# Attention and projections with split words on one core: order of the weight pieces on ScalarE, first queries by another queue, flag made at step 88

## The chip, the cores and the metric

One core of a Trainium2 chip runs the whole program. The metric is the device time of one execution in microseconds; the time of a kernel is the median over several runs. The core has five engines, each with its own order of instructions that is fixed when the program is built: TensorE (PE, matrix products), VectorE (DVE), ScalarE (ACT), GpSimd (POOL) and SyncE (SP, which here only issues transfers). SP and ScalarE each have a queue for transfers. Engines wait for each other by semaphores; an instruction that waits holds up everything behind it on its engine.

## The reference

Four batches of 768 tokens, eight heads of 64. Attention is local and causal (a token sees itself and the `n_local` - 1 = 95 tokens before it) with the first `n_global` = 8 tokens visible to all, and a bias that falls with distance. Its output, 3072 rows of 512, goes through two products with a GELU between them:

```python
scores = scale * np.matmul(q, k.transpose(0, 1, 3, 2)) + bias
scores = np.where(keep, scores, -1000000000.0)
a = softmax(scores)                       # with 1e-9 in the denominator
x = (a @ v).transpose(0, 2, 1, 3).reshape(3072, 512)
h = x @ w_in                              # 512 -> 2048
g = 0.5 * h * (1.0 + erf(h / sqrt(2)))
out = (g @ w_out).astype(float32)         # 2048 -> 512
```

`n_local`, `n_global`, `w_in` and `w_out` come as 64-bit numbers, so the weights are 16 MB of words.

## The kernel before, in words

The 3072 tokens are cut into 12 chunks of 256 (three to a batch), and the 2048 middle columns into 8 slices of 256. A *step* `T` is one chunk with one slice: `m1` (line 461) multiplies the chunk's `x` with the slice of `w_in` into `h`, `gelu` (lines 471 to 473) takes ScalarE, GpSimd and VectorE in turn, and `m2` (line 491) multiplies with the slice of `w_out` and adds up in `acc`. There are 96 steps. The first 16 take chunks 0 and 1 by turns, slice after slice, so that the weights are needed slowly at first; from step 16 on a chunk takes its eight slices in a row.

Products are made in a fast number format, with each operand split into a high part `h` and a low part `l` and three products added (`wh*xh + wh*xl + wl*xh`). The names in the profile follow this: `winh`, `winl`, `wouth`, `woutl`, `xh`, `xl`, `gh`, `gl`.

**Attention** of a chunk is spread over about ten steps (`att`): scores `s` (line 332 for the first two chunks, called native because their attention isn't split; line 336 for the others), exponentials on ScalarE (line 356), a transpose `t` on TensorE (line 382) that ScalarE copies to `pt` (line 385 or 389), the product `av` with the values (line 410 or 424), and `x`. The attention of chunk 0 and chunk 1 comes ahead of step 0 for the most part. Its loads are kr (keys), qr (queries) and vr (values), for four pairs of heads each, all issued by SP (lines 225 to 229 and 286 to 293). The load of the limits (line 55) stands between them, and the masks `pen` are made from it.

**Weights** come in 32 pieces, four to a slice (two of `w_in`, two of `w_out`), each a transfer of 512 KB (line 156), with four buffers for slices 0 to 6. A piece is turned from 64-bit words into a high and a low part in six operations (`split_weights`, lines 180 to 193):

- ScalarE, line 180: the low words, in place, to integers of a few bits. This is the first ScalarE operation of a piece, and it waits for the load.
- VectorE, lines 182 and 184: bits of the high words into `wb`.
- VectorE, line 186: `wb` and the low words joined. After it the buffer is free, and SP can issue the load of a later piece.
- ScalarE, line 192: the high part `hi` (winh or wouth).
- VectorE, line 193 (the page shows line 151): the low part `lo`.

Slice `s` is split at step `DECODE[s]` (-6, -4, ... 8) in the order of the program text. That text isn't the order of the engines: a planner orders each engine's instructions when the program is built, by when it thinks their inputs are ready and then by their place in the text. `after` (line 134) gives it an extra edge between two instructions. Such an edge is an order, not a transfer of data: between two instructions of one engine it becomes no semaphore. The kernel uses it to keep the loads of the weights in order and to keep exponentials and GELUs in order.

**The flag.** The fast path holds only for limits of a certain size, moderate scores and moderate weights. All words of the weights are therefore loaded a second time (`check_load`, `c` in the profile) during steps 16 to 80, and VectorE folds them into `wand` (line 203). At the end `flag` (line 578) folds all conditions into one number `flag_i`: ten small VectorE operations, a TensorE transpose of one column (line 596) and three more VectorE operations. One of its tiles, `wmin`, has the tag "o", whose two buffers are also those of the output tiles. Each engine then reads the number (line 750) and branches (line 751) past the general path, which isn't run on these inputs.

Of the kernel before, what the change touches and what calls it, by code (L numbers as in the profile page):

```python
# [10 lines left out]
I32 = mybir.dt.int32  # L11
# [6 lines left out]
P = 128  # L18
# [5 lines left out]
CT = 256  # L24
# [27 lines left out]

def load_scalars(nc, pool, src, name):
    w = pool.tile([P, 2, 2], I32, name=name + "_w")
    nc.sync.dma_start(w.rearrange("p i t -> p (i t)"), src.bitcast(I32).partition_broadcast(P))
    f = pool.tile([P, 2, 2], F32, name=name + "_f")
    nc.vector.tensor_copy(f, w)
    r = pool.tile([P, 2], F32, name=name)
    lo, hi = f[:, :, 0], f[:, :, 1]
    nc.vector.scalar_tensor_tensor(out=r, in0=lo, scalar=0.0, in1=hi, op0=ALU.is_lt, op1=ALU.add)  # L60
    nc.vector.scalar_tensor_tensor(out=r, in0=r, scalar=4294967296.0, in1=lo, op0=ALU.mult, op1=ALU.add)
    return r[:, 0:1], r[:, 1:2]
# [6 lines left out]
class Fast:  # L69
    def __init__(self, tc, ctx, qT, kT, v, w, out, limits):  # L70
        self.tc, self.nc = tc, tc.nc
        self.qT, self.kT, self.v, self.w, self.out = qT, kT, v, w, out
        self.limits = limits
        pool = lambda name, bufs=1, **k: ctx.enter_context(tc.tile_pool(name=name, bufs=bufs, **k))
        self.ctx = ctx
        self.early = ExitStack()
        self.es = self.early.enter_context(tc.tile_pool(name="es", bufs=1, side="right"))
        self.const = pool("const")
        self.wts = pool("wts")
        self.stg = pool("stg", 3)  # L80
        self.kq = pool("kq", 2)
        self.vp = pool("vp", 2)
        self.pp = pool("pp", 4)
        self.ptp = pool("ptp", 2)
        self.xp = pool("xp", 3)
        self.gp = pool("gp", 2)
        self.sm = pool("sm", 2)
        self.words = ExitStack()
        self.ws = self.words.enter_context(tc.tile_pool(name="ws", bufs=4))
        self.ps_acc = pool("ps_acc", 2, space=PSUM)  # L90
        self.ps = pool("ps", 6, space=PSUM)
        self.win, self.wout = {}, {}
        self.kt, self.qt, self.vt, self.raw = {}, {}, {}, {}
        self.pt_n, self.pt_t, self.av, self.x = {}, {}, {}, {}
        self.stat, self.g, self.h = {}, {}, {}
        self.acc, self.t3 = {}, {}
        self.xs = {}
        self.last_table = self.last_word = None

    def consts(self):  # L100
        nc, const = self.nc, self.const
# [65 lines left out]
    def split_weights(self, s):  # L167
        nc = self.nc
        if s == LATE:
            self.early.close()  # L170
            self.wts = self.ctx.enter_context(self.tc.tile_pool(name="wlate", bufs=1, side="right"))
        if s == NST - 1:
            self.words.close()
            self.wts = self.ctx.enter_context(self.tc.tile_pool(name="wlast", bufs=1))
        for nm, dst, shape in (("win", self.win, [P, 4, 256]), ("wout", self.wout, [P, 2, 512])):
            dst[s] = tuple(self.wts.tile(shape, F32R, name=f"{nm}{k}{s}") for k in "hl")
        for i in range(4):
            w = self.raw.pop((s, i, "w"))
            lw, hw = w[:, :, 0], w[:, :, 1]
            nc.scalar.activation(out=lw, in_=lw.bitcast(U32), func=AF.Copy, scale=2.0 ** -29)  # L180
            a = self.sm.tile([P, 512], I32, name=f"wb{s}_{i}", tag="o")
            nc.vector.tensor_scalar(out=a, in0=hw, scalar1=0x07FFFFFF, scalar2=3,
                                    op0=ALU.bitwise_and, op1=ALU.logical_shift_left)
            nc.vector.scalar_tensor_tensor(out=a, in0=hw, scalar=-0x40000000, in1=a,  # L184
                                           op0=ALU.bitwise_and, op1=ALU.bitwise_or)
            nc.vector.tensor_tensor(out=a, in0=a, in1=lw, op=ALU.add)  # L186
            af = a.bitcast(F32)
            if i < 2:
                hi, lo = (x[:, 2 * i:2 * i + 2, :].rearrange("p d f -> p (d f)") for x in self.win[s])
            else:  # L190
                hi, lo = (x[:, i - 2, :] for x in self.wout[s])
            nc.scalar.copy(hi, af)
            self.lo_dve(lo, af, hi)

    def check_load(self, n):
# [19 lines left out]
    def load_qk(self, c, p):  # L215
        nc = self.nc
        b, cc = divmod(c, CPB)
        k0 = (b * H + 2 * p) * D * S
        first = cc == 0
        nb = 1 if first else 2  # L220
        if c in NATIVE:
            kr = self.es.tile([P, nb, 256], F32, name=f"kr{c}_{p}", tag="kn", bufs=4)
            qr = self.es.tile([P, CT], F32, name=f"qr{c}_{p}", tag="qn", bufs=4)
            if first:
                nc.sync.dma_start(kr[:, 0, :], dap(self.kT, k0, [[S, P], [1, 256]]))
            else:
                nc.sync.dma_start(kr[:, :, NG:256], dap(self.kT, k0 + cc * CT - 96, [[S, P], [P, 2], [1, 224]]))
                nc.sync.dma_start(kr[:, :, 0:NG], dap(self.kT, k0, [[S, P], [0, 2], [1, NG]]))
            nc.sync.dma_start(qr, dap(self.qT, k0 + cc * CT, [[S, P], [1, CT]]))
            self.raw[c, p] = (kr, qr, nb)  # L230
            return
        if p == 0 and (cc == 1 or c == len(NATIVE)):
            self.load_glob(b)
        kr = self.stg.tile([P, 2, nb, 256], F32, name=f"kr{c}_{p}", tag="stage", padded_shape=[P, 2, 2, 256])
        qr = self.stg.tile([P, 2, CT], F32, name=f"qr{c}_{p}", tag="qraw", bufs=1)
        for u in (0, 1):
            ps = slice(u * 64, u * 64 + 64)
            if first:
                nc.sync.dma_start(kr[ps, :, 0, :], dap(self.kT, k0, [[S, D], [D * S, 2], [1, 256]]))
            else:  # L240
                for j in range(2):
                    nc.sync.dma_start(
                        kr[ps, :, j, NG:256],
                        dap(self.kT, k0 + cc * CT + j * P - 96, [[S, D], [D * S, 2], [1, 224]]))
            nc.sync.dma_start(qr[ps], dap(self.qT, k0 + cc * CT, [[S, D], [D * S, 2], [1, CT]]))
        self.raw[c, p] = (kr, qr, nb)
# [285 lines left out]
                    if r == rr:  # L532
                        self.exps(c, bt)

    def run(self):
        self.load_qk(0, 0)
        self.consts()
        last = NCH * NST
        for c in NATIVE:
            for p in range(NP):  # L540
                if (c, p) != (0, 0):
                    self.load_qk(c, p)
                self.load_v(c, p)
            if c == 0:
                for s in range(3):
                    self.load_weights(s)
        for s in range(3, NST - 1):
            self.load_weights(s)
        for self.T in range(START[0] - 1, last):
            T = self.T  # L550
            for s in range(NST):
                if T == DECODE[s]:
                    if s == NST - 1:
                        self.load_weights(s)
                    self.split_weights(s)
            if 16 <= T < 80 and T % 2 == 0:
                self.check_load((T - 16) // 2)
            if 18 <= T < 82 and T % 2 == 0:
                self.check_words((T - 18) // 2)
            if 0 <= T + 1 < last:  # L560
                self.m1(T + 1, 0)
            self.att(T, "pt", 0)
            if 0 <= T + 1 < last:
                self.m1(T + 1, 1)
                self.gelu(T + 1)
            self.att(T, "s", 0)
            self.att(T, "pt", 1)
            if T >= 0:
                self.m2(T, 0)
            self.att(T, "av", 0)  # L570
            self.att(T, "s", 1)
            self.att(T, "exp", 0)
            self.att(T, "split", 0)
            if T >= 0:
                self.m2(T, 1)
            self.att(T, "av", 1)
# [164 lines left out]
def body(tc, qT, kT, v, w, limits, out):  # L741
    nc = tc.nc
    w = w.bitcast(I32)
    with tc.tile_pool(name="flagp", bufs=1) as fp:
        flag_i = fp.tile([1, 1], I32, name="flag_i")
        with ExitStack() as ctx:
            fast = Fast(tc, ctx, qT, kT, v, w, out, limits)
            fast.run()
            fast.flag(flag_i)
        fv = nc.values_load(flag_i, min_val=0, max_val=1)  # L750
        with tc.If(fv):
            general(tc, qT, kT, v, w, out, limits)
# [25 lines left out]
```

## Time and profile before

| what | value |
|---|---|
| median of 3 runs | 751.67 us (749.25 to 754.20) |
| profiled execution | 753.28 us |
| its span, from the first to the last instruction | 750.9 us |
| granted TensorE clock, mean | 0.991 |
| busy: TensorE, VectorE, ScalarE, GpSimd | 718.8, 502.2, 355.6, 304.0 us |
| moved by DMA | 80.91 MB |

A row of a timeline gives the start and the duration in microseconds, the engine, the line, the operation, the tile written and the tiles read, their shapes, the number of instructions merged, and in square brackets how long the engine stood idle before it and what released it. An engine's name with a q (SPq, ACTq, PEldq) is its sequencer, which issues transfers, reads registers and branches. In rows with three numbers divided by slashes these are shortest, median and longest in nanoseconds, followed by the start of the first and the last in microseconds. PEld is the load of the stationary operand, which overlaps the products.

### The profile page before, as it was taken

The numbers are of one execution on the slowest core, as the hardware profiler recorded it, in microseconds if no ns is written. First come the engines' busy times: TensorE is split into PE (matmuls) and PEld (weight loads), VectorE is DVE, ScalarE is ACT, GpSimd is POOL, SyncE is SP. The second block draws the span as 40 slices with busy tenths as digits, with TensorE's granted clock in tenths as the row PEclk, the third lists the DMA queues.
The fourth block names the chain that finished last, engine by engine and source line by source line (L and its number), as shares of the span: only waits on it lengthen the run. The fifth ranks groups of instructions, "written<-read, shape, count | busy, mean of one in ns | idle before, by whom it ended". The sixth has DMA issues, their size and how long they took to land.

```text
span 750.9 us, 13415 instructions
## 1 busy us (share of the span) xinstructions
PE 718.8 (96%) x4617; PEld 649.8 (87%) x4617; DVE 502.2 (67%) x1317; ACT 355.6 (47%) x906; POOL 304.0 (40%) x572
## 2 busy tenths in 40 slices
PE   5997989898999999999999999999999999999995
PEld 3776989787999999999889999999889999989984
DVE  6888887756857867856757867856658867633111
ACT  5646545455355355355355355355355455351110
POOL 2220033654544654543544554542533654431010
PEclk9999999999999999999999999999999999999998
DMA  8995523324434434334424434334334431100000
GB/s 245 269 242 176 173 81 113 98 64 120 119 101 137 115 101 127 97 88 132 119 82 136 119 101 122 100 92 124 99 103 117 127 110 43 44 15 1 29 1 32
DMA packets 74395, 80.91 MB, mean 108 GB/s; under 512 B 12368, under 2 KB 63056, under 8 KB 74320
## 3 DMA queue, kind: packets, MB, share of 16 engines
q1 hardware_dynamic: 70864, 73.69, 34.9%
q10 hardware_dynamic: 3456, 6.29, 2.3%
q8 instruction: 38, 0.62, 0.3%
q14 instruction: 37, 0.30, 0.1%
HBM read 73.66 MB, written 6.29 MB: 106 GB/s over the span
## 4 chain that ended last, share of the span: by engine, by line
PE 69%; DMA 10%; DVE 6%; ACT 6%; POOL 4%; issue 2%; SPq 1%; DVEq 0%; POOLq 0%; ACTq 0%
PE acc L491 29%; PE h L461 27%; DMA w<-w 7%; PE av L424 4%; PE s L336 4%; PE t L382 4%; POOL n L369 3%; ACT n L356 3%; DMA c<-w 2%; DMA kr<-kT 1%; POOL gh L145 1%; DVE wb L186 1%; ACT L356 1%; DVE wb L184 1%; ACT gr L471 1%
## 5 line engine op out<-in xcount | busy, mean ns | idle before, releaser
L461 PE MATMUL h<-xh,winh 128*128 128x256 f32 x768 | 219.7, 286 | 0.0
L461 PE MATMUL h<-xl,winh 128*128 128x256 f32 x768 | 218.6, 285 | 0.0
L461 PE MATMUL h<-xh,winl 128*128 128x256 f32 x768 | 217.3, 283 | 0.0
L491 PE MATMUL acc<-wouth,gh 128*128 128x512 f32 x384 | 155.0, 404 | 7.4 <-POOL gh L145 7.4
L491 PE MATMUL acc<-woutl,gh 128*128 128x512 f32 x384 | 152.4, 397 | 0.0
L461 PEld LDWEIGHTS h<-xh,winh 128*128 128x128 f32 x768 | 146.9, 191 | 2.4
L461 PEld LDWEIGHTS h<-xl,winh 128*128 128x128 f32 x768 | 146.9, 191 | 2.1
L461 PEld LDWEIGHTS h<-xh,winl 128*128 128x128 f32 x768 | 146.9, 191 | 0.2
L491 PE MATMUL acc<-wouth,gl 128*128 128x512 f32 x384 | 144.1, 398 | 1.2 <-DVE gl L151 1.2
L151 DVE TENSOR_TENSOR gl<-gr,gh 128x512 fp32r<-128x512 f32 x96 | 68.6, 715 | 92.5 <-POOL gh L145 92.5
L471 ACT ACTIVATE gr<-h 128x512 f32<-128x512 f32 x96 | 57.4, 598 | 149.8 <-PE h L461 109.9
L369 POOL TENSOR_SCALAR n<-n,su 128x256 f32<-128x256 f32 (+1 forms) x160 | 77.5, 504 | 87.7 <-DVE su L361 76.4
L145 POOL TENSOR_SCALAR gh<-gr 128x512 fp32r<-128x512 f32 x96 | 65.4, 681 | 108.9 <-ACT gr L471 108.9
L145 POOL TENSOR_SCALAR vt<-vr 128x256 fp32r<-128x256 f32 (+1 forms) x80 | 34.7, 435 | 154.1 <-DMA vr<-v 79.5
L356 ACT ACTIVATE n<-n,mn 128x256 f32<-128x256 f32 (+1 forms) x192 | 91.8, 480 | 7.8 <-DVE mn L341 7.5
L491 PEld LDWEIGHTS acc<-wouth,gh 128*128 128x128 f32 x384 | 73.2, 191 | 20.3 <-POOL gh L145 9.2
L491 PEld LDWEIGHTS acc<-wouth,gl 128*128 128x128 f32 x384 | 73.0, 190 | 18.2 <-DVE gl L151 2.9
L491 PEld LDWEIGHTS acc<-woutl,gh 128*128 128x128 f32 x384 | 73.2, 191 | 12.5
L431 ACT COPY t<-av 64x256 f32<-64x256 f32 x80 | 29.3, 366 | 99.3 <-PE av L424 98.8
L389 ACT CAST pt<-t 128x512 fp32r<-128x512 f32 (+1 forms) x80 | 44.4, 555 | 65.0 <-PE t L382 59.4
L341 DVE CUSTOM_DVE_ANT_0 n<-s,pen 128x256 f32<-128x256 f32 (+1 forms) x192 | 68.4, 391 | 5.1 <-PE s L336 3.5
L382 PE MATMUL t<-ident,n 128*128 128x128 f32 x352 | 61.2, 295 | 1.3 <-ACT gr L471 0.7
(87 smaller groups left out, 1060.9 us busy)
## 6 DMA issues: line engine op xcount, KB each, us to landing
w<-w SPq DMA_DIRECT2D x32, 512.0 KB, 4.6
c<-w SPq DMA_DIRECT2D x32, 512.0 KB, 3.7
kr<-kT SPq DMA_DIRECT2D x112, 112.0 KB, 2.7
qr<-qT SPq DMA_DIRECT2D x88, 128.0 KB, 3.1
vr<-v SPq DMA_DIRECT2D x48, 128.0 KB, 2.3
out<-o ACTq DMA_DIRECT2D x24, 256.0 KB, 2.2
kr<-kT SPq DMA_DIRECT2D x28, 128.0 KB, 2.8
vr<-v SPq DMA_DIRECT2D x32, 96.0 KB, 2.2
```

The source lines that it names most:

```text
L145: self.nc.gpsimd.tensor_scalar(out=out, in0=in_, scalar1=scale, scalar2=0.0, op0=ALU.mult, op1=ALU.add)
L151: self.nc.vector.tensor_tensor(out=out, in0=in_, in1=hi.bitcast(F32), op=ALU.subtract)
L336: nc.tensor.matmul(sp[:, j, :w], lhsT=qq[:, hh, j * P:(j + 1) * P], rhs=kt[:, t, 0 if first else j, :w], start=t == 0, stop=t == 1)
L341: nc.vector.tensor_tensor_reduce(out=nn[:, j, :w], in0=sp[:, j, :w], in1=pen, scale=-slope(h), scalar=3e38, op0=ALU.add, op1=ALU.min, accu ...
L356: ins = nc.scalar.activation(out=nn[:, j, :w], in_=nn[:, j, :w], func=AF.Exp, bias=mn[:, i:i + 1], scale=-1.0, accum_out=su[:, i:i + 1])
L369: nc.gpsimd.tensor_scalar(out=nn[:, j, :w], in0=nn[:, j, :w], scalar1=su[:, i:i + 1], scalar2=0.0, op0=ALU.mult, op1=ALU.add)
L382: nc.tensor.transpose(tp[:, i, :], nn[:, j, a * P:(a + 1) * P], self.ident)
L389: nc.scalar.copy(pt[:, :, 0, :], tp[:, :n, :])
L424: nc.tensor.matmul(av[:, j], lhsT=vt[:, vi], rhs=pt[:, i], start=start, stop=stop)
L461: nc.tensor.matmul(hp[:, f, :], lhsT=w[:, d, f * P:(f + 1) * P], rhs=x[:, d, :], start=n == 0, stop=n == 3 * NP - 1)
L471: self.table(nc.scalar.activation(out=gr, in_=hp, func=AF.Gelu))
L491: nc.tensor.matmul(acc, lhsT=g[:, f, ks], rhs=w[:, f, :], start=s == 0 and n == 0, stop=s == NST - 1 and n == 5)
```

## The change: an edge between weight pieces, five loads on ScalarE's queue, the flag made earlier

Three edits:

1. Line 180 of every piece but the first gets an edge to line 192 of the piece before it: ScalarE begins a piece only when it has made the high part of the one before. The edge joins two instructions of the same engine.
2. The load of the limits, and the four query loads of chunk 0, are issued by ScalarE instead of SP. They are then in ScalarE's order and on its queue.
3. `flag` is called in the loop at `T == 88`, ahead of `m1` of step 89, instead of after the last step. At that point the last words have been folded into `wand` (step 80), the output tiles of chunk 10 have been written (step 87), and those of chunk 11 have not.

```diff
 def load_scalars(nc, pool, src, name):
     w = pool.tile([P, 2, 2], I32, name=name + "_w")
-    nc.sync.dma_start(w.rearrange("p i t -> p (i t)"), src.bitcast(I32).partition_broadcast(P))
+    nc.scalar.dma_start(w.rearrange("p i t -> p (i t)"), src.bitcast(I32).partition_broadcast(P))
...
-        self.last_table = self.last_word = None
+        self.last_table = self.last_word = self.last_hi = None
...
-            nc.scalar.activation(out=lw, in_=lw.bitcast(U32), func=AF.Copy, scale=2.0 ** -29)
+            ins = nc.scalar.activation(out=lw, in_=lw.bitcast(U32), func=AF.Copy, scale=2.0 ** -29).ins
+            if self.last_hi is not None:
+                self.after(ins, self.last_hi, "a piece begins when ScalarE is through with the one before")
...
-            nc.scalar.copy(hi, af)
+            self.last_hi = nc.scalar.copy(hi, af).ins
...
-            nc.sync.dma_start(qr, dap(self.qT, k0 + cc * CT, [[S, P], [1, CT]]))
+            (nc.scalar if c == 0 else nc.sync).dma_start(qr, dap(self.qT, k0 + cc * CT, [[S, P], [1, CT]]))
...
-    def run(self):
+    def run(self, flag_i):
...
+            if T == 88:
+                self.flag(flag_i)
...
-            fast.run()
-            fast.flag(flag_i)
+            fast.run(flag_i)
```

## The prediction

> **What bounds the kernel now.** I read the page first, then the busy time by stretches, then the waits and single engines inside the stretches that lose time, and last the end of the span.
>
> ```profile
> PE 718.8 (96%) x4617; PEld 649.8 (87%) x4617; DVE 502.2 (67%) x1317; ACT 355.6 (47%) x906; POOL 304.0 (40%) x572
> ```
>
> TensorE is busy 718.8 of 750.9 us, so 32 us at most can come from closing its gaps. By stretches (columns: stretch, its length, busy us of PE, PEld, DVE, ACT and POOL, granted clock, DMA share, GB/s):
>
> ```profile
> 0.00:10.00 10.00, 4.73 (x21) 2.98 (x21) 5.65 (x32) 3.27 (x10) 4.12 (x20) 1.00 0.62 187
> 10.00:20.00 10.00, 7.73 (x26) 5.09 (x25) 7.99 (x28) 8.14 (x25) 0.81 (x2) 1.00 1.00 312
> 40.00:50.00 10.00, 10.00 (x35) 8.00 (x34) 8.82 (x25) 5.46 (x15) 2.50 (x4) 1.00 0.97 239
> 50.00:60.00 10.00, 8.00 (x28) 5.59 (x27) 7.36 (x20) 5.93 (x15) 1.42 (x2) 1.00 0.96 262
> 60.00:70.00 10.00, 7.16 (x28) 5.81 (x27) 8.44 (x26) 6.89 (x19) 0.36 (x1) 1.00 0.47 147
> 90.00:100.00 10.00, 8.05 (x58) 7.39 (x57) 8.39 (x15) 5.07 (x9) 1.53 (x2) 1.00 0.55 179
> 200.00:350.00 150.00, 150.00 (x1019) 138.44 (x1018) 110.86 (x293) 72.03 (x191) 75.02 (x141) 1.00 0.40 113
> ```
>
> From 200 to 350 us TensorE never stops, and no edit touches that part. What can be won lies in two places: the first 100 us (idle 5.27 + 2.27 + 2.00 + 2.84 + 1.95 = 14.3 us in the rows shown), and what comes after TensorE's last product. What ends the early waits:
>
> ```profile
> ACT w L180 <- DMA w<-w: 31.6, 20, 2.7
> PE av L410 <- ACT pt L385: 7.5, 4, 3.2
> ```
>
> These are the waits of the first 130 us (total, times, longest). ScalarE stands still 31.6 us at line 180, the first operation of a weight piece, because the piece has not landed. What stands behind it in ScalarE's order waits too, and TensorE waits for such work. The place where it hurts most, ScalarE first and then TensorE:
>
> ```profile
> 65.30 0.68 ACT L180 ACTIVATE w<-w 128x512 int32<-128x512 uint32 x1 [1.03 <-DMA w<-w]
> 67.93 0.67 ACT L180 ACTIVATE w<-w 128x512 int32<-128x512 uint32 x1 [1.95 <-DMA w<-w]
> ...
> 69.75 0.56 ACT L385 COPY pt<-t 128x512 f32<-128x512 f32 x1
> 70.22 0.62 ACT L192 CAST winh<-wb 128x512 fp32r<-128x512 f32 x1
> 70.74 0.62 ACT L192 CAST wouth<-wb 128x512 fp32r<-128x512 f32 x1
> ```
> ```profile
> 70.37 1.97 PE L410 MATMUL av<-vr,pt 128*128 128x64 f32 x8 [3.21 <-ACT pt L385]
> 97.39 0.50 PE L491 MATMUL acc<-wouth,gh 128*128 128x512 f32 x1 [1.95 <-POOL gh L145]
> ```
>
> The copy of the probabilities stands behind two line-180 operations that waited 1.03 and 1.95 us, and TensorE lost 3.21 us. Note also the order: counted from the start, the operations at 65.30 and 67.93 are the 16th and 17th of line 180, those at 70.22 and 70.74 the 14th and 15th of line 192. ScalarE begins pieces two ahead of the one it finishes.
>
> **Part 1, the order of pieces.** The edge adds no instruction and no semaphore, only an order on one engine: line 180 of a piece after line 192 of the piece before. The two operations above move behind 70.74 us, and the copy at 69.75 no longer has them ahead of it. By the time line 180 comes up, its piece has mostly landed, so the 31.6 us of standing still shrink. The cover for delaying the pieces is their lead:
>
> ```profile
> L180 ACT ACTIVATE w<-w x32: 645/680/716, 13.0 to 134.9; 128x512 int32<-128x512 uint32 x32
> ```
> ```profile
> 178.64 0.60 ACT L471 ACTIVATE gr<-h 128x512 f32<-128x512 f32 x1 [2.51 <-PE h L461]
> ```
>
> The last piece is begun at 134.9 us; the 15th GELU, the first that needs its slice (step 14), starts at 178.64. Less the 5 us or so that finishing the piece takes, the lead is nearly 40 us.
>
> What TensorE can win is bounded by the idle of 50 to 70 us and of 90 to 100 us, 2.00 + 2.84 + 1.95 = 6.8 us. Below, it can cost: the new order is a chain through two engines, priced as a rival. I take 4 us. It is nearer to the full sum, because the longest gap (3.21) lies directly behind the moved operations. It is not all of it, because a VectorE that is this full will be late next:
>
> ```profile
> 10.00:70.00 60.00, 52.90 (x183) 40.44 (x181) 50.44 (x149) 38.48 (x108) 11.29 (x18) 1.00 0.91 249
> 10.00:110.00 100.00, 90.53 (x429) 75.44 (x428) 86.24 (x214) 60.84 (x148) 16.50 (x24) 1.00 0.71 204
> ```
>
> **Part 2, queries and limits by ScalarE's queue.** The diff moves five issues off SP: four query loads and the limits. Before:
>
> ```profile
> 1.22 0.42 SPq L229 DMA_DIRECT2D qr<-qT  x1
> 1.67 0.44 SPq L55 DMA_DIRECT2D nn_w<-limits  x1
> ...
> 7.01 2.10 SPq L156 DMA_DIRECT2D w<-w  x4
> ```
> ```profile
> 13.00 0.68 ACT L180 ACTIVATE w<-w 128x512 int32<-128x512 uint32 x1 [1.23 <-DMA w<-w]
> 14.09 1.54 PE L410 MATMUL av<-vr,pt 128*128 128x64 f32 x6 [2.27 <-ACT pt L385]
> ```
>
> Each issue costs SP about 0.45 us with its gap, so everything behind moves up by 5 x 0.45 = 2.2 us, the first weight loads from 7.01 to about 4.8. On ScalarE the five issues take the same 2.2 us ahead of its first exponential, and it has only 3.27 us of work in the first 10. The 2.27 us that TensorE lost before 14.09 hang on a copy behind line 180, which hung on the first weight piece; the query and the limits themselves come perhaps 0.5 us sooner. Upper bound 2.2 + 0.5 = 2.7 us. Lower bound: a loss of about 1 us if the queries come up behind other work on ScalarE. The DMA share is 1.00 in the next ten microseconds and 0.97 still at 40 to 50, so earlier issues only help as far as they fill the unused 0.38 of the first ten. I take 1.5 us.
>
> The Trainium skill (Trainium Kernel Development and Optimization, Key Constraints) says that issuing from several engines saves only the sequencer's issue time, since all queues share the same 16 DMA engines. By it alone the gain would end at the 2.2 us of issue time and could be nothing at a share of 1.00; the sum above keeps both ends anyway.
>
> **Part 3, the flag.** The end of the run as it is:
>
> ```profile
> 741.02 0.39 PE L491 MATMUL acc<-wouth,gl 128*128 128x512 f32 x1
> 742.21 0.34 ACTq L498 DMA_DIRECT2D out<-o  x1
> 743.35 0.29 DVE L590 CAST wmin<-wand 128x256 f32<-128x256 int32 x1 [5.43 <-DMA out<-o]
> 745.42 0.14 DVE L600 CAST flag_i<-red 1x1 int32<-1x1 f32 x1
> ```
> ```profile
> 741.15 2.07 DMA out<-o
> ```
> ```profile
> L750 PEldq TENSOR_LOAD <-flag_i x1: 494/494/494, 745.6 to 745.6; - x1
> ```
> ```profile
> L751 PEldq COMPARE_BRANCH x1: 3514/3514/3514, 746.2 to 746.2; - x1
> L751 PEldq EVENT_SEMAPHORE  x1: 51/51/51, 749.8 to 749.8; - x1
> ```
>
> Today the flag's last stretch waits for an output store, because `wmin` takes a buffer of the tag that the output tiles rotate through. It ends at 745.56. Only then can each engine read the flag (0.49 us) and branch, and TensorE's branch takes 3.51 us. Nothing but closing semaphores follows it, 749.7 to 750.9 = 1.2 us. With the flag made eight steps earlier, TensorE reads it right after its last product: 741.41 + 0.49 + 0.1 + 3.51 + 1.2 = 746.7, a gain of 4.2 us. The last store, issued at 742.21, lands near 744.4 and lies beside that branch. If the branch too is hidden, the store is what is late next: 744.4 + 1.2 = 745.6, a gain of 5.3. If every engine waits for that store before it reads the flag, the 5.3 us from 745.56 to 750.9 follow 744.4, a gain of 1.2. I take 4.2, since the rows give each engine its own read and branch.
>
> What the flag costs where it goes:
>
> ```profile
> 698.54 0.34 ACTq L498 DMA_DIRECT2D out<-o  x1
> 703.48 0.69 DVE L151 TENSOR_TENSOR gl<-gr,gh 128x512 fp32r<-128x512 f32 x1 [4.92 <-POOL gh L145]
> ```
>
> `wmin` now waits for the store of the chunk before, landed at about 698.54 + 2.1 = 700.7. Its three followers run until about 701.9. Behind them on VectorE stands only the next `gl` at 703.48, so VectorE hides this. TensorE gets one small transpose, and whoever is queued behind it waits if it is placed before 701.9: between 0 and 2.8 us (from 699.1, where step 87 ends). I take 0.4, because the order comes from a planner that places an operation when its inputs are due.
>
> **Sum.** 4 + 1.5 + 4.2 - 0.4 = 9.3 us. The profiled execution took 753.28 us (span 750.9 and 2.4 us around it), which gives 744.0. It lay 1.6 us above the median of the runs, 751.67; from the median the sum gives 742.4. I say 742.5 us.
>
> **Rivals.**
>
> *Only the tail moves (20%).* TensorE's early gaps are filled by VectorE's lateness: between 10 and 110 us VectorE has 13.8 us free, and if the copies come sooner but the exponentials' inputs do not, gaps only change their owner. Against it: the gap at 70.37 has ScalarE as its releaser, not VectorE. Time: 4.2 - 0.4 and about 0.5 for the start, 751.67 - 4.3 = 747.4.
>
> *All early gaps go (8%).* 6.8 + 2.7 + 4.2 = 13.7, so 738, or below if the waits before 10 us shrink too, about 735.
>
> *The pieces become a serial chain (10%), on the slower side.* The other of its two ScalarE operations, and the 28th piece:
>
> ```profile
> 103.15 0.68 ACT L180 ACTIVATE w<-w 128x512 int32<-128x512 uint32 x1 [1.46 <-DMA w<-w]
> ```
> ```profile
> L192 ACT CAST winh<-wb x16: 602/608/623, 16.1 to 132.2; 128x512 fp32r<-128x512 f32 x16
> ```
>
> VectorE's join of a piece (line 186) needs line 180, which now needs line 192, which needs the join before. Between two joins lie 0.61 + 0.68 = 1.3 us of ScalarE. VectorE has the next piece's masks and the last piece's low part to do meanwhile; where the order does not offer them, it stands still with GELU low parts and scores behind it. If all 1.3 us showed for the 28 pieces begun by 104 us, 36 us would meet 13.8 us of slack: 22.6 later, less 5.3 of the other parts, 769. It cancels every gain when (13.8 + 5.3) / 28 = 0.68 us show per piece, and makes the kernel more than 1% slower at 0.95. For it speaks VectorE's fill of 86%; against it, that the pieces have nearly 40 us of lead, so that most of such delay falls on work that nobody awaits. I give 6% to beyond 1%, 4% to the stretch below it.
>
> *The first chunks run at TensorE's faster pace (3%).* Two groups of the same eight products:
>
> ```profile
> 64.50 1.81 PE L410 MATMUL av<-vr,pt 128*128 128x64 f32 x8
> 78.65 1.00 PE L410 MATMUL av<-vr,pt 128*128 128x64 f32 x8
> ```
>
> The granted clock is given as 1.00 throughout, yet the products got nearly twice as fast shortly after the dense projections began. If closing the gaps brought the fast pace to the first chunks, TensorE would need 45% less there and VectorE would bound: its free 60 - 50.44 = 9.6 us between 10 and 70 are the most, giving 742.4 - 9.6 = 733. The Trainium skill (TensorE: Matmul & The Clock Gate, Part 1) lets the clock rise after some 3.4 us of sustained work. By that rule it should have risen in 40 to 50 us already, where the row shows 10.00 busy; the trace disagrees, hence 3%.
>
> *The flag does not leave the end (3%).* If reading it stays tied to the end of all work, the tail gains 1.2 and the transpose costs up to 2.8: about 747.8 with the early parts.
>
> That leaves 56% for the forecast, 738 to 747.
>
> **The numbers.** About 1% (7.5 us) is what a measurement of this kernel can tell from no change; the border lies at 744.2. Of the forecast's 56% I put 42 below it; with all gaps gone and the faster pace that is 0.53 faster. Same: 14 + 20 + 3 + 4, 0.41. Slower: 0.06. The range, 735.5 to 750, leaves out the faster pace, the lowest gaps-gone cases, the slow side and the ends of the others.
>
> **What would show it.** Right: in the changed profile lines 180 and 192 alternate on ScalarE, the wait of line 180 for the DMA falls from 31.6 to under 15 us, the gap of 3.21 us is gone, the first weight load is issued near 4.8 us, and the span ends about 5.3 us after the last product instead of 9.5. Wrong: VectorE waiting at line 186 for line 180 by more than 10 us in total, TensorE's busy share of 50 to 100 us no higher, a TensorE wait of over 1 us at line 596, or engines that read the flag only after the last store.

## The result, and the profile after

| | before | after |
|---|---|---|
| median (runs of one comparison) | 752.71 us (749.25 to 754.20, 4 runs) | 740.42 us (739.55 to 742.29, 4 runs) |
| profiled execution, its span | 753.28, 750.9 us | 739.55, 737.5 us |
| granted TensorE clock, mean | 0.991 | 0.998 |

The changed kernel is faster by 12.3 us: a ratio of 0.9846, with a 95% interval of 0.9818 to 0.9875. Its line numbers are two higher from line 182 on (192 is now 194, 385 is 387, 461 is 463) and three higher at the end (750 is 753).

The first part of the page, busy time by engine, and then the busy time by stretches, with the columns as before:

```profile
PE 715.7 (97%) x4617; PEld 647.1 (88%) x4617; DVE 504.1 (68%) x1317; ACT 355.2 (48%) x906; POOL 309.7 (42%) x572
```
```profile
0.00:10.00 10.00, 4.05 (x18) 2.38 (x19) 5.51 (x30) 2.50 (x6) 4.29 (x20) 1.00 0.71 200
50.00:60.00 10.00, 10.00 (x36) 7.88 (x36) 9.94 (x31) 7.67 (x22) 0.88 (x1) 1.00 0.83 259
60.00:70.00 10.00, 9.31 (x39) 8.28 (x40) 8.84 (x22) 6.70 (x15) 1.31 (x2) 1.00 0.62 190
90.00:100.00 10.00, 9.67 (x65) 8.78 (x65) 9.90 (x17) 5.62 (x10) 2.25 (x3) 1.00 0.59 181
```

The three stretches on which the prediction counted (50 to 60, 60 to 70 and 90 to 100 us) had 6.8 us of idle TensorE; now it is 1.0. The first ten microseconds have more idle than before (5.95 against 5.27). TensorE also needs 3.1 us less busy time for the same 4617 products (715.7 against 718.8).

The waits of the first 130 us (engine, tile and line that wait, what ends the wait; total, times, longest):

```profile
ACT w L180 <- DMA w<-w: 1.2, 1, 1.2
PE av L412 <- ACT pt L387: 2.9, 2, 2.2
ACT wouth L194 <- DVE wb L188: 15.5, 9, 3.2
ACT winh L194 <- DVE wb L188: 11.2, 11, 2.0
```

ScalarE no longer stands in front of a load (31.6 us before, 1.2 now). It has not become free: it now waits 26.7 us for VectorE's join, against 8.4 before. ScalarE's timeline where the prediction quoted that of before:

```profile
61.97 0.62 ACT L194 CAST winh<-wb 128x512 fp32r<-128x512 f32 x1 [1.07 <-DVE wb L188]
62.50 0.68 ACT L180 ACTIVATE w<-w 128x512 int32<-128x512 uint32 x1
...
64.24 0.62 ACT L194 CAST winh<-wb 128x512 fp32r<-128x512 f32 x1 [0.81 <-DVE wb L188]
64.77 0.69 ACT L180 ACTIVATE w<-w 128x512 int32<-128x512 uint32 x1
...
65.84 0.58 ACT L387 COPY pt<-t 128x512 f32<-128x512 f32 x1
```
```profile
66.47 3.67 PE L412 MATMUL av<-vr,pt 128*128 128x64 f32 x16 [0.69 <-ACT pt L387]
70.22 0.56 PE L463 MATMUL h<-xh,winh 128*128 128x256 f32 x1
```

Lines 194 and 180 alternate, line 180 finds its words landed, and TensorE's gap of 3.21 us has become 0.69.

The start, SP's waits up to 12 us and its first weight load:

```profile
SPq L288 <- DMA vr<-v: 1.0, 1, 1.0
SPq L227 <- DMA qr<-qT: 1.0, 1, 1.0
SPq L288 <- DMA kr<-kT: 0.6, 1, 0.6
```
```profile
6.83 2.07 SPq L156 DMA_DIRECT2D w<-w  x4
```

Before, SP issued its 13 loads without a wait and reached the weights at 7.01. With five issues fewer it waits 2.6 us for landings and reaches them at 6.83. ScalarE, which now makes those five issues, starts its first exponential at 8.72 us instead of 7.95.

The end: TensorE's last product and ScalarE's last store in the timelines, then ScalarE's read of `flag_i` and the branches (durations in nanoseconds, then the start):

```profile
731.13 0.39 PE L493 MATMUL acc<-wouth,gl 128*128 128x512 f32 x1
```
```profile
732.32 0.34 ACTq L500 DMA_DIRECT2D out<-o  x1
```
```profile
L753 ACTq TENSOR_LOAD <-flag_i x1: 477/477/477, 732.7 to 732.7; - x1
```
```profile
L754 PEldq COMPARE_BRANCH x1: 3417/3417/3417, 728.7 to 728.7; - x1
L754 ACTq COMPARE_BRANCH  x1: 54/54/54, 733.2 to 733.2; - x1
L754 ACTq EVENT_SEMAPHORE  x1: 17/17/17, 735.9 to 735.9; - x1
```

The flag is made beside the products (`wmin` at 690.56 us, waiting for a store as before, with nothing behind it that is late). From the end of the last product (731.52) to the end of the span are 5.98 us, against 9.49. TensorE's sequencer read the flag at 728.1 us and branched at 728.7, while queued products still ran. ScalarE is what is late now: it reads after its last store, and its next instruction comes 2.65 us after a branch that itself takes 54 ns.

### The profile page after: what moved, and what is told of

Read it like the earlier page. It is cut to its first block, busy times and chain, and to the rows that moved or that the text cites. A ratio compares the mean times of both kernels' runs of the same rounds, so it can differ in the third digit from the quotient of the medians.

```text
span 737.5 us, 13431 instructions
## 1 busy us (share of the span) xinstructions
PE 715.7 (97%) x4617; PEld 647.1 (88%) x4617; DVE 504.1 (68%) x1317; ACT 355.2 (48%) x906; POOL 309.7 (42%) x572
## 4 chain that ended last, share of the span: by engine, by line
PE 71%; DVE 10%; DMA 7%; POOL 5%; ACT 4%; issue 3%; SPq 1%; ACTq 0%; DVEq 0%; POOLq 0%
PE acc L493 29%; PE h L463 29%; PE av L426 4%; PE s L338 4%; PE t L384 4%; POOL n L371 3%; DMA w<-w 3%; DMA vr<-v 2%; DMA c<-w 2%; ACT n L358 2%; DVE wb L188 1%; DVE wb L186 1%; DVE n L343 1%; POOL gh L145 1%; DVE wb L184 1%
## 5 line engine op out<-in xcount | busy, mean ns | idle before, releaser
L493 PEld LDWEIGHTS acc<-woutl,gh 128*128 128x128 f32 x384 | 72.5, 189 | 12.3
```

Of the source, the lines that this page charges most:

```text
L493: nc.tensor.matmul(acc, lhsT=g[:, f, ks], rhs=w[:, f, :], start=s == 0 and n == 0, stop=s == NST - 1 and n == 5)
```

## The experiments

Each kernel was timed beside the kernel before, in three groups in which that one took 752.48, 752.61 and 753.00 us. To see where time goes *within* a run I use one marker, the start of ScalarE's GELU of a step, since TensorE hardly stops once the steps run. From ScalarE's timeline of the profiled executions, in us ("edge and flag" and "the change" were each profiled twice, and both are listed):

| kernel | step 0 | step 16 | step 95 | span ends |
|---|---|---|---|---|
| before | 80.8 | 192.7 | 735.9 | 750.9 |
| flag alone | 82.8 | 194.3 | 734.5 | 745.6 |
| queue edit alone | 84.8 | 198.0 | 738.0 | 753.0 |
| edge alone | 75.5 | 185.5 | 725.4 | 740.6 |
| edge and flag | 73.6, 75.9 | 183.3, 185.7 | 722.9, 726.9 | 734.7, 738.5 |
| edge, flag, queries | 75.3 | 185.0 | 724.4 | 736.2 |
| edge, flag, limits | 76.3 | 185.9 | 727.2 | 738.7 |
| the change | 76.6, 75.6 | 186.1, 185.3 | 726.0, 726.2 | 737.5, 737.3 |
| first piece too, edge, flag | 76.9 | 186.5 | 727.9 | 740.0 |
| last stores on SP, edge, flag | 76.8 | 186.4 | 727.1 | 739.1 |
| edge two back, flag | 77.9 | 188.5 | 729.7 | 741.5 |
| line 180 on GpSimd, flag | 76.8 | 192.6 | 734.4 | 745.4 |

Two executions of one kernel differ by up to 4 us here (edge and flag: 722.9 and 726.9), so only larger differences, or means over several, are read.

**The edge alone.** Edits 2 and 3 are left out.

```diff
-            nc.scalar.activation(out=lw, in_=lw.bitcast(U32), func=AF.Copy, scale=2.0 ** -29)
+            ins = nc.scalar.activation(out=lw, in_=lw.bitcast(U32), func=AF.Copy, scale=2.0 ** -29).ins
+            if self.last_hi is not None:
+                self.after(ins, self.last_hi, "a piece begins when ScalarE is through with the one before")
...
-            nc.scalar.copy(hi, af)
+            self.last_hi = nc.scalar.copy(hi, af).ins
```

> Only the edge between weight pieces. Theory 'standing behind loads': the whole gain up to TensorE's last product comes from here, so about 10 us less than before (741 to 744 against 752.7), the wait of ScalarE's line 180 for the loads falls from 33 us to a few, and TensorE's gap of 3.2 us is gone. Rival 'new planning': the gain belongs to the combination, because every edit gives another order; alone the edge gives under 5 us.

Measured: 742.29 us (4 runs), ratio 0.9856 (0.9822 to 0.9889), 10.2 us less. Line 180 waits 0.8 us for loads. The edge alone gives most of the result, and about two and a half times what the prediction took for it.

**The queue edit alone.**

```diff
-    nc.sync.dma_start(w.rearrange("p i t -> p (i t)"), src.bitcast(I32).partition_broadcast(P))
+    nc.scalar.dma_start(w.rearrange("p i t -> p (i t)"), src.bitcast(I32).partition_broadcast(P))
...
-            nc.sync.dma_start(qr, dap(self.qT, k0 + cc * CT, [[S, P], [1, CT]]))
+            (nc.scalar if c == 0 else nc.sync).dma_start(qr, dap(self.qT, k0 + cc * CT, [[S, P], [1, CT]]))
```

> Only the limits and the first queries on ScalarE's queue. From the changed profile, where SP waits for landings before it issues the third key load and the first weight load comes at 6.83 instead of 7.01: between 0 and 1 us slower than before, the first exponential about 0.8 us later. The prediction's own term said 1.5 us faster. Rival 'new planning': any sign, by 3 us or more.

Measured: 755.65 us (10 runs), ratio 1.004 (1.002 to 1.006): 3.2 us *more*. SP's waits up to 12 us, and the waits of the first 130 us:

```profile
SPq L286 <- DMA vr<-v: 1.3, 1, 1.3
SPq L286 <- DMA kr<-kT: 0.7, 1, 0.7
SPq L225 <- DMA qr<-qT: 0.7, 1, 0.7
```
```profile
ACT w L180 <- DMA w<-w: 33.0, 19, 4.2
PE av L410 <- ACT pt L385: 10.9, 4, 6.2
```

SP's five issues saved are spent on waits for landings, and the weights start no sooner (7.04 against 7.01). TensorE's wait for the copies rises from 7.5 to 10.9 us, with a single one of 6.2. That one ends with a copy at 53.15 us, behind a line 180 that had waited 2.43 us for its load. This points to ScalarE's standing in front of loads, and beside the edge the same edit costs nothing (below). But the loss is over three times the most that was expected here and as large as the rival's, a new order by the planner, which isn't excluded. Why a small shift of the start makes one of those waits so long isn't settled.

**The flag alone.**

```diff
+            if T == 88:
+                self.flag(flag_i)
...
-            fast.run()
-            fast.flag(flag_i)
+            fast.run(flag_i)
```

> Only the flag at step 88. The tail from TensorE's last product to the end shrinks from 9.5 to about 6.0 us as in the changed kernel, all else stays: 3 to 4 us faster than before (about 749). Rival: the transpose holds up TensorE at step 88, then 1 us or less is left.

Measured: 747.89 us (5 runs), ratio 0.9945 (0.9919 to 0.9972), 4.6 us less. From the last GELU to the end of the span it takes 11.1 us (745.6 - 734.5), the kernel before 15.0. At steps 0 and 16 it isn't ahead of the kernel before.

Its trace also shows a cost that the prediction had no term for, and that the kernel before has at another place (see Part 1 below). TensorE after a gap at 98 us, and the stretches there (the column after the five engines is the granted clock):

```profile
99.54 0.70 PE L491 MATMUL acc<-wouth,gh 128*128 128x512 f32 x1 [1.80 <-POOL gh L145]
```
```profile
100.00:102.00 2.00, 2.00 (x8) 1.69 (x7) 2.00 (x5) 1.48 (x3) 0.24 (x1) 0.50 0.00 0
102.00:104.00 2.00, 2.00 (x14) 2.00 (x14) 1.97 (x4) 0.83 (x2) 0.64 (x1) 0.73 0.61 186
```

After a gap of 1.80 us TensorE works at a granted 0.50 for some 3 us: a product of `m2` takes 0.63 us there and 0.40 once the clock is back. With the 0.92 of the two microseconds before, it is short by 2 x (0.08 + 0.50 + 0.27) = 1.7 us at full clock, nearly as much again as the gap.

**Edge and flag, without the queue edit.** The diffs of the first and the third kernel together.

> The edge and the flag, without the queue edit. If the queue edit costs, this is 0 to 1 us faster than the changed kernel's 740.4 (739.5 to 740.5), and the first exponential starts at 7.95 again. If the queue edit is worth its 1.5 us, 742. Rival 'new planning': off by 3 us or more either way.

Measured: 740.14 us (4 runs), ratio 0.9842 (0.9814 to 0.9870). It was run a second time in the third group.

> The kernel of e4_edge_flag once more, beside the changed kernel on the same chip, for the worth of the queue edit when the edge is there: 740, first weight load at 7.0 us.

Measured there: 740.43 us (5 runs), ratio 0.9836 (0.9818 to 0.9855). That is the changed kernel's time without the queue edit. Beside the flag alone the edge is worth 7.6 us (747.89 to about 740.3), and beside the edge alone the flag is worth 2.0 (742.29 to 740.3), while each alone gave 10.2 and 4.6. The two don't quite add up; with medians of four and five runs, each spread over 3 to 5 us, I make nothing of the difference. In the profiles the flag shortens the way from the last GELU to the end by about 3.5 us beside the edge as well: 15.2 us with the edge alone, 11.6 and 11.8 with both.

**The edge two pieces back.** With the flag; line 180 follows line 192 of the piece before the previous one, so ScalarE may be one piece ahead.

```diff
+            if self.older_hi is not None:
+                self.after(ins, self.older_hi, "a piece begins when ScalarE is through with the one before")
...
+            self.older_hi, self.last_hi = self.last_hi, nc.scalar.copy(hi, af).ins
```

> Edge to the piece before the last one (ScalarE may begin one piece ahead), with the flag at step 88. Theory 'standing behind loads': part of the standing comes back, line 180 waits for loads for 8 to 25 us in the first 130, time between e4_edge_flag and e3_flag, 742 to 746. Rival 'the strict order as such' (one piece at a time spares VectorE and the buffers): then there is nothing between, and it stays within 1 us of one of the two.

Measured: 741.28 us (4 runs), ratio 0.9835 (0.9793 to 0.9877). The waits of the first 130 us:

```profile
ACT w L180 <- DMA w<-w: 6.4, 7, 2.6
```

Line 180 stands 6.4 us instead of 1.1 with the strict edge and the flag, less than the 8 to 25 expected, and TensorE waits longer for its copies (6.2 us against 3.6). The four runs lie apart, two at 739.0 and 739.1 and two at 743.4 and 744.8; the profiled one is of the slower pair and reaches step 16 3 us later than the strict edge does on average. So the median can't be told from that of the strict edge, and four runs don't say whether the looser edge costs something. Most of the gain is there without the order being one piece at a time.

**Line 180 on GpSimd.** With the flag, without the edge. This tells apart whether the gain comes from the order of the pieces as such or from ScalarE not standing in front of a load.

```diff
-            nc.scalar.activation(out=lw, in_=lw.bitcast(U32), func=AF.Copy, scale=2.0 ** -29)
+            nc.gpsimd.tensor_scalar(out=lw, in0=lw.bitcast(U32), scalar1=2.0 ** -29, scalar2=0.0,
+                                    op0=ALU.mult, op1=ALU.add)
```

> No edge; line 180 is done by GpSimd instead of ScalarE, flag at step 88. Theory 'standing behind loads': ScalarE has nothing left that waits for a weight load ahead of its copies, so TensorE's waits for pt (9.3 us in e3_flag) fall below 4 us and the time comes near e4_edge_flag, 739 to 744, unless GpSimd standing behind the loads holds up the GELU's high parts. Rival 'the strict order as such': the time stays at e3_flag's 748.

Measured: 748.19 us (5 runs), ratio 0.9936 (0.9903 to 0.9968); one of the five took 1374.75 us, which the ratio leaves out and nothing explains. Its waits of the first 130 us, GpSimd's timeline at one place, and TensorE's longest gap after step 0:

```profile
POOL w L180 <- DMA w<-w: 33.8, 20, 4.8
```
```profile
130.22 0.75 POOL L180 TENSOR_SCALAR w<-w 128x512 int32<-128x512 uint32 x1 [2.58 <-DMA w<-w]
```
```profile
131.64 0.44 PE L383 MATMUL t<-ident,n 128*128 128x128 f32 x2 [2.25 <-POOL n L370]
```

The 33.8 us of standing still haven't gone; they have moved to another engine. At step 0, before which GpSimd has little else to do, this kernel is 6.0 us ahead of the flag alone (76.8 against 82.8) and 4.0 ahead of the kernel before, as the edge is. The lead over the flag alone is still 7.0 us at step 7 (119.2 us); by step 10 it is down to 1.6, and the total is that of the flag alone. Between these steps GpSimd waits 4.80, 3.62 and 2.58 us at line 180, and the scaling of the exponentials (`n`, line 370), for which TensorE waits, starts at 131.06 us, right behind the last of them. After that gap the granted clock is 0.50 for two microseconds. So in this execution too the harm is done where an engine stands in front of a load with other work behind it, though the engine is another one.

**The first piece too.** Edge and flag, with an extra edge: the first piece's line 180, the only one that still waits for its load (1.1 us), follows the second copy of chunk 0.

```diff
-            nc.scalar.copy(pt, tp[:, :n, :])
+            ins = nc.scalar.copy(pt, tp[:, :n, :]).ins
+            if (c, h) == (0, 1):
+                self.last_hi = ins
```

> Edge and flag as in e4_edge_flag, and the first piece's line 180, which has no predecessor, is tied behind the second copy of the transposed probabilities. Theory 'standing behind loads': the last gap of this kind, TensorE's 2.1 us before 14 us, shrinks to under 1 us and the whole is 1 to 1.5 us faster than e4_edge_flag. Rival: the first piece's delay is handed on to the later pieces and the buffers, no difference.

Measured: 741.43 us (5 runs), ratio 0.9831 (0.9805 to 0.9857). TensorE's wait for the copies falls from 3.6 to 2.0 us and the time doesn't: step 0 starts at 76.9. So something else must be late there; what it is wasn't looked for.

**The last stores on SP.** Edge and flag, with chunk 11's stores issued by SP, so that ScalarE needn't issue them before it reads the flag.

```diff
-            nc.scalar.dma_start(self.out[r:r + P, :], o)
+            (nc.sync if c == NCH - 1 else nc.scalar).dma_start(self.out[r:r + P, :], o)
```

> Edge and flag as in e4_edge_flag, and the output tiles of the last chunk are stored by SP's queue. Theory on the tail: after the change ScalarE is the last to read the flag, since its last store's issue stands ahead of the read, and its way through the branch ends 3.3 us after that issue. With the store on SP, ScalarE can read and branch while its last copy waits, and the last landing sets the end: 1 to 2 us less than e4_edge_flag, TensorE's last product to the end 4.5 us instead of 6.0. Rival: SP takes its place with the same read and branch behind the issue, then no difference.

Measured: 741.02 us (5 runs), ratio 0.9838 (0.9811 to 0.9865): no gain. ScalarE's last copy, then its read, and what follows its branch and SP's:

```profile
732.66 0.59 ACT L499 COPY o<-acc 128x512 f32<-128x512 f32 x1 [0.32 <-PE acc L493]
```
```profile
L753 ACTq TENSOR_LOAD <-flag_i x1: 473/473/473, 732.7 to 732.7; - x1
```
```profile
L754 SPq EVENT_SEMAPHORE  x8: 17/17/17, 734.2 to 737.7; - x8
L754 ACTq EVENT_SEMAPHORE  x1: 17/17/17, 736.3 to 736.3; - x1
```

ScalarE reads the flag when its last copy has started, not before. TensorE's early read in the changed kernel isn't an exception: it comes at 728.1 us, as the last `gl` that its products wait for ends (727.35 + 0.69), and what still runs then is products that wait for nothing. From ScalarE's branch at 733.2 to its next instruction are 3.1 us here. SP, behind the two stores, branches at 733.7, and the last of its rows at line 754 starts at 737.7, 1.4 us after ScalarE's. So SP has taken ScalarE's place at the end, much as the rival said (only its read comes early, at 693.9).

**The queue edit in two.** Edge and flag, with the queries alone on ScalarE's queue, and with the limits alone.

```diff
-            nc.sync.dma_start(qr, dap(self.qT, k0 + cc * CT, [[S, P], [1, CT]]))
+            (nc.scalar if c == 0 else nc.sync).dma_start(qr, dap(self.qT, k0 + cc * CT, [[S, P], [1, CT]]))
```

> Edge and flag, and of the queue edit only the four queries on ScalarE's queue. Theory 'the issuers wait for each other's landings': SP again waits about 2.5 us in the first 7 us for loads that ScalarE issued, and the first weight load is issued near 6.8 us, not at the 5.2 us that the issue times alone would give. Rival 'issue time only': no such wait, first weight load near 5.2. Total within 2 us of e4_again.

```diff
-    nc.sync.dma_start(w.rearrange("p i t -> p (i t)"), src.bitcast(I32).partition_broadcast(P))
+    nc.scalar.dma_start(w.rearrange("p i t -> p (i t)"), src.bitcast(I32).partition_broadcast(P))
```

> Edge and flag, and of the queue edit only the limits on ScalarE's queue. Theory 'the issuers wait for each other's landings': with one load on the other queue at most one wait of SP, the first weight load between 6.5 and 7.0 us. Total within 2 us of e4_again.

Beside them the changed kernel was run again.

> The changed kernel beside e4_again. The queue edit alone cost 3.2 us; if that cost came from ScalarE standing longer behind loads, the edge takes it away and this is within 1 us of e4_again. If it came from the start of the run itself, this is 2 to 4 us slower than e4_again.

Measured: queries 739.70 us (4 runs), ratio 0.9825 (0.9797 to 0.9853); limits 739.72 us (4 runs), ratio 0.9825 (0.9809 to 0.9841). In the same group edge and flag alone took 740.43 us, and the changed kernel 739.92 us (5 runs; ratio 0.9839, 0.9817 to 0.9862). All four lie within 0.8 us. SP's waits up to 12 us with the queries moved, its first weight load there, and that with the limits moved:

```profile
SPq L288 <- DMA vr<-v: 1.0, 1, 1.0
SPq L288 <- DMA qr<-qT: 0.9, 1, 0.9
SPq L288 <- DMA nn_w<-limits: 0.3, 1, 0.3
```
```profile
7.07 1.89 SPq L156 DMA_DIRECT2D w<-w  x4
```
```profile
6.56 2.20 SPq L156 DMA_DIRECT2D w<-w  x4
```

Moving one load takes one issue off SP, and the weights come 0.45 us sooner (6.56 against 7.01). Moving four saves four issues, 1.8 us, and SP waits 2.2. Neither reaches the end of the run.

## Why the prediction was right, and where it wasn't

The forecast was 742.5 us, from a sum of 9.3; measured were 740.4 and 12.3. Of its three terms one was far too small, one brought nothing or a loss, and one fits in size. That the total came out so near is in part luck, since two of the errors cancel.

**Part 1 had the right mechanism and the wrong size.** All that it named came: the waits of line 180 went, the lines alternate, the gap became 0.69. Its 4 us, bounded by 6.8, measured 10.2 alone and 7.6 beside the flag. In the table the mean over the nine executions with the edge to the piece before is 75.8 us at step 0 and 185.5 at step 16; before and the flag alone average 81.8 and 193.5. So 6.0 us are won ahead of the first GELU, 2.0 more by step 16, and nothing that could be told from chance after that. Sorted by what TensorE did up to step 16, these 8.0 us are 5.6 us less idle, which the bound of 6.8 allowed, and 2.4 us less busy time for the same 959 products, for which the prediction had no term. The step that failed is the bound: "What TensorE can win is bounded by the idle of 50 to 70 us and of 90 to 100 us". Idle is not all that can be won, because the pace of the products changes too. Two things lie outside the prediction's reading.

First, TensorE's clock. After some gaps the granted clock drops, so that such a gap costs its length and a stretch at half pace behind it. The kernel before shows it at 136 us:

```profile
136.76 0.50 PE L491 MATMUL acc<-wouth,gh 128*128 128x512 f32 x1 [2.06 <-POOL gh L145]
```
```profile
136.00:138.00 2.00, 1.24 (x4) 0.96 (x5) 1.49 (x3) 0.13 (x2) 1.24 (x2) 0.83 0.00 0
138.00:140.00 2.00, 2.00 (x6) 1.58 (x6) 2.00 (x7) 1.80 (x5) 0.62 (x1) 0.50 0.06 18
140.00:142.00 2.00, 2.00 (x12) 1.72 (x11) 2.00 (x4) 0.13 (x1) 0.08 (x1) 0.81 0.36 113
```

2 x (0.17 + 0.50 + 0.19) = 1.7 us lost there, and as much at 100 us with the flag alone. None of the nine executions with the edge has a row below 1.00 between steps 0 and 16. It doesn't follow every gap: behind that of 1.95 us at 97 us, in the kernel before, the clock stays at 1.00. I had read the mean clock of 0.991 and priced nothing for it. The mean alone would not have given the price either: 0.9% of 750.9 us is 6.8 us, but only 3.4 of it lie ahead of the last product, 1.7 here and 1.7 at 530 us. The Trainium skill (TensorE: Matmul & The Clock Gate, Part 1) has the clock halve after an idle window of about 3.4 us. The runs differ in this: gaps of 1.80 and 2.06 us were followed by 0.50. By that figure alone these gaps would have been free of it.

Second, the first GELU stood behind line 180 as well, in ScalarE's timeline of before:

```profile
78.82 0.70 ACT L180 ACTIVATE w<-w 128x512 int32<-128x512 uint32 x1 [1.20 <-DMA w<-w]
...
80.83 0.60 ACT L471 ACTIVATE gr<-h 128x512 f32<-128x512 f32 x1
```

The first `h` began at 72.41 then and at 70.22 now, 2.2 us sooner; the first GELU came at 80.83 then and at 76.59 now, 4.2 us sooner. The last product of that `h`, in TensorE's timeline of before and of after:

```profile
78.09 0.28 PE L461 MATMUL h<-xh,winl 128*128 128x256 f32 x1
```
```profile
74.64 0.28 PE L463 MATMUL h<-xh,winl 128*128 128x256 f32 x1
```

So of the other 2.0 us, 1.2 were won on TensorE (before, eight late `av` products and some transposes lay between the two halves of `h`, now only transposes) and 0.8 on ScalarE, where line 180 no longer waits ahead of the GELU. The prediction, which looked at the copies alone, didn't follow what else stood in ScalarE's queue. This is one pair of executions; how the gain divides over the other steps was not separated.

**Part 2 was wrong.** Taken at a gain of 1.5 us, it costs 3.2 alone and nothing that can be told from zero beside the edge (739.92 against 740.43). The step that failed: "everything behind moves up by 5 x 0.45 = 2.2 us, the first weight loads from 7.01 to about 4.8". They moved to 6.83. The 0.45 us for each issue was right (the limits alone show it: 6.56), but the prediction took SP's issues as if they waited for nothing. With four loads on another queue SP waited 2.2 us for landings, with five 2.6 and 2.7. The lower bound of -1 us wasn't low enough for the edit alone. It priced only the start, and the harm shows in TensorE's waits for ScalarE's copies (10.9 us against 7.5), which the edge shortens; that this is all of it was argued, not shown. What makes SP wait for landings once two queues are in use isn't shown by a trace, beyond that it does.

**Part 3 was right in size and wrong about what is late.** Taken at 4.2 - 0.4 = 3.8 us; the profiles show 9.49 - 5.98 = 3.5, the flag alone 4.6. The flag left the end, and no engine waited for the last store before it read. But TensorE's branch, which the sum put last, is hidden: its sequencer began it at 728.7, 2.8 us before the last product ended. ScalarE's branch took its place, nearly as long. The rows of before gave a hint of it:

```profile
L751 ACTq COMPARE_BRANCH  x1: 54/54/54, 746.1 to 746.1; - x1
...
L751 ACTq EVENT_SEMAPHORE  x1: 17/17/17, 749.8 to 749.8; - x1
```

After its branch of 54 ns ScalarE, too, took until 749.8, and VectorE the same. I had read TensorE's as the longest one because its duration is shown on the branch and ScalarE's isn't. The 0.4 us for the transpose wasn't needed; no wait of TensorE at it appears.

**The rivals.** *Only the tail moves* fell: the edge alone gives 10.2 us. *A serial chain* didn't come, though its links exist: ScalarE waits 26.7 us for joins, but in the trace of after VectorE doesn't wait at its join (line 186, now 188) for line 180, and the delayed pieces are awaited by nobody. *All early gaps go* described the gaps from 50 to 100 us rightly; its time of 738 or below counted a gain of 2.7 at the start that didn't come. *A faster pace in the first chunks* didn't come in the profiled execution: the products turn fast at 72.7 us, 2.5 us after the first dense one, and not before. In five of the nine executions with the edge, a second one of the changed kernel among them, it came for a moment. Eight `av` products of edge and flag, second execution:

```profile
65.14 1.00 PE L412 MATMUL av<-vr,pt 128*128 128x64 f32 x8
```

Then the granted clock fell to 0.63 and 0.52 (68 to 72 us), and the pace was slow again until the dense products had run for some 2 us.

The sum fell short because a term that was 3.6 to 6.2 us too small stood against one that was only 1.5 us too large.

**Left open.** Before's profiled execution is 3 us slower than that with the flag alone between steps 16 and 95 (543.2 against 540.2). The trace shows where: a gap of 1.73 us that ends at 529.58 us, with granted clocks of 0.97, 0.50 and 0.68 in the six microseconds from 528 on, 1.7 us lost. No other execution listed has a row below 1.00 between these steps. Why this one has it isn't shown.

## What to carry to other kernels

When an engine with work in order shows many short waits for a load at one line, don't price the line but everything that stands behind it: move the line back until the data is there, even if that engine then waits longer elsewhere. Moving the wait to another engine helps only as long as that engine has nothing urgent behind it. Price a TensorE gap with the half-pace stretch that can follow it, and a move of loads to a second queue with the landings that the first queue then waits for, not with issue time alone.

## What the runs showed of the hardware

- A TensorE gap of 2.06 us (before, 136 us) was followed by granted clocks of 0.83, 0.50 and 0.81 over six microseconds, one of 1.80 us (flag alone, 99 us) by 0.92, 0.50 and 0.73, with 1.7 us lost each time. One of 1.95 us (before, 97 us) was followed by 1.00.
- The products of the first chunks run at about half pace at a granted clock given as 1.00; that column doesn't show this state. TensorE's timeline of after, where it ends:

```profile
72.50 0.41 PE L463 MATMUL h<-xl,winh 128*128 128x256 f32 x1
...
73.68 0.28 PE L463 MATMUL h<-xh,winh 128*128 128x256 f32 x1
```

The products of one shape take 0.41 us and then 0.28; their starts are 0.21 us apart at first and 0.12 then. With the flag alone the same products take 0.41 us between 74 and 77 us, and there the column says 0.50.

- A branch costs an engine far more than the record of it: on ScalarE 54 ns, and 2.65 us (the change), 3.1 (last stores on SP) and 3.6 (before) until the next instruction; on TensorE 3.4 us within the record. The Trainium skill (Runtime: NRT & Kernel Launch, Instruction fetch mechanics) says that a taken branch to a page that isn't loaded has to fetch it first. The durations agree with a cost of that kind. The DMA rows of the changed kernel have one transfer of the kind "instruction" between 733.2 and 736 us, after ScalarE's branch; that ScalarE waits for it isn't shown.
- TensorE's sequencer read a register 3.4 us ahead of the end of its queued products (728.1 against 731.52), as soon as the last tile that they wait for was made (728.04). ScalarE's read came as its last copy, which had waited, started (732.7 and 732.66).
